# wq's guest rows in four loads of 9, 3, 7 and 5 rows from two queues, instead of eight loads of three rows from one

## The chip, the cores and the metric

The kernel runs on one core of a Trainium2 chip. The core has five engines that work side by side and meet at semaphores: TensorE (PE in the profile), VectorE (DVE), ScalarE (ACT), GpSimd (POOL) and SyncE (SP). Sixteen DMA engines bring data from HBM, the chip's main memory, into SBUF, the core's memory of 128 partitions. SP, ScalarE and GpSimd can each put loads into a queue of their own, and the same 16 DMA engines serve all queues. The metric is device time in microseconds (us), lower is better.

## The reference

One decode step of a transformer block for 4 sequences, all in float32: a layer norm whose scale and shift come from a condition c, attention over the last 2048 positions of a key and value cache, and a gated feed-forward part.

```python
mod = (_silu(c) @ w_mod).reshape(c.shape[0], 6, 1, -1)
sa, ca, ga, sb, cb, gb = (mod[:, n] for n in range(6))
h = _layernorm(x) * (1 + ca) + sa
# attention: 32 query heads, 8 key/value heads, window W = 2048, Dh = 128
q = (h @ wq) ...
o = softmax(q k^T * Dh ** -0.5) v
x = x + ga * (o @ wo)
h = _layernorm(x) * (1 + cb) + sb
x = x + gb * ((_silu(h @ w1) * (h @ w3)) @ w2)
```

With only 4 tokens there is little arithmetic for each weight and each cache entry: keys and values are 67 MB, the weights some 34 MB, and each of these bytes is used once.

## The kernel before, in words

**Memory.** `ring` is one SBUF tensor of three slots; a slot holds 128 partitions of 16384 floats, 8.39 MB. Every large load goes to a slot or a part of one, one row to each partition: w_mod_a (the part of w_mod that the first norm needs, with x and c), wq, seven loads kv_in (keys and values of one key/value head for all four sequences), wo_mod, the last head's keys with a quarter of wo (last_k_wo), its values (last_v), another quarter of wo, w1, w3, and w2 in four pieces of falling size.

**The order of the loads.** `load` (L174) issues a DMA on SP's queue unless told otherwise. SP issues w_mod_a, then the guest loads (below), then kv_in 0 to 6 and the rest in the order above. ScalarE issues one load, wq (L188), at the start. A load into a slot in use waits until the engines have read what lies there; `Program` (L44) finds such waits from the partitions and columns that each instruction touches, and gives every DMA a semaphore of its own.

**Guests.** wq as laid out on the host has 128 rows of 16384 floats. The last 240 columns (`GUESTS`) of every row are cut off, so that the load of wq has 128 rows of 16144 floats. The pieces that were cut off travel as an input of their own, `guests`: 24 rows of 6 x 240 = 1440 floats, in which a piece of six different partitions stands in one row. They are loaded into partitions 0 to 11 and 32 to 43 of the tile p_sb, which the softmax uses later; GpSimd clears those partitions first (L200). The eight loads before are written

```python
for m in range(2):
    for c in range(4):
        do("sync", "dma_start", guest[32 * m + c : 32 * m + 12 : 4], guests[12 * m + c : 12 * m + 12 : 4])
```

so each has the three partitions 32m + c, 32m + c + 4 and 32m + c + 8. In the matmuls with hT and wq (L306 to L315) the last 240 columns are taken from there: six matmuls with a matching slice `hg` of the transposed activations add the guests' share (twelve records in the trace, since a float32 matmul runs in two passes).

**Compute.** The first norm and its modulation wait for w_mod_a. Then come q (wq), and for each key/value head: scores on TensorE into s_ps, a maximum on VectorE (nm), the exponential on ScalarE (p_sb), transposes (bank), and the product with the values (o_ps). `project_out` multiplies by wo. At the end the feed-forward part runs twice through `ffn_in`, for w1 and for w3, and then through w2, whose last pieces are consumed as they land. The program's marked line splits it into two parts for its semaphores; the change lies in the first.

**Engines beside the stream.** On GpSimd there are five clearing instructions for tiles around the guest loads (p_sb, sc, hidT, qT, xs), and later one copy of x into xs, which waits for w_mod_a.

Of the kernel before, what the change touches and what calls it, by code (L numbers as in the profile page):

```python
# [147 lines left out]
def block_kernel(nc, w_mod_a, wq, guests, kv_in, wo_mod, last_k_wo, last_v, wo, w1, w3, w2, out):  # L148
# [5 lines left out]
    do = Program(nc)  # L154
# [19 lines left out]
    def load(dst, src, cuts=(0, 1), queue="sync"):  # L174
        step = src.shape[1] // cuts[-1]
        for lo, hi in zip(cuts[:-1], cuts[1:]):
            do(queue, "dma_start", dst[:, lo * step : hi * step], src[:, lo * step : hi * step])
        return dst[:, : src.shape[1]]
# [20 lines left out]
    p_all = sb("p_sb", NT * 512)  # L199
    do("gpsimd", "memset", p_all[:44], 0.0)  # L200
    guest = p_all[:44, : 6 * GUESTS]
    for m in range(2):
        for c in range(4):
            do("sync", "dma_start", guest[32 * m + c : 32 * m + 12 : 4], guests[12 * m + c : 12 * m + 12 : 4])
    kv[0] = load(slots[2], kv_in[0])
    sc = sb("sc", 4, 32)
    do("gpsimd", "memset", sc, 0.0)
# [98 lines left out]
    for half in range(2):  # L306
        qp = s_ps[half]
        for k in range(4):
            for i in range(4):
                at = ((half * 4 + i) * 4 + k) * 512  # L310
# [228 lines left out]
```

## Time and profile before

| | |
|---|---|
| time, median of 3 runs | 242.16 us (242.08 to 242.38) |
| span of the profiled execution, first to last instruction | 240.8 us |
| PE busy | 148.7 us (62%) |
| DVE busy | 56.3 us (23%) |
| ACT busy | 24.1 us (10%) |
| POOL busy | 4.5 us (2%) |
| mean granted TensorE clock | 0.865 |
| HBM read | 101.22 MB |

The page gives no time of its own for the profiled execution beside its span; the runs' median is 1.36 us above that span. The profile's lines name an instruction's source line, engine and operation, then the tile written and the tiles read. Nearly all compute has the line L59, that of the helper that records every operation, so groups are told apart by their tiles. A row of the timeline begins with its start and its length in us; what stands in square brackets is how long the engine was idle before it and what ended that. In the windows every engine has its busy time and, in brackets, its instructions; then come the granted clock, the mean busy share of the 16 DMA engines, and GB/s. A packet belongs to the window in which it starts, so a share over a short window can be a little off, and even above 1.

### The profile page before, as it was taken

The page shows a single profiled execution, that of the slowest core. Times are in us where ns is not written, and L with a number is a line of the kernel's source. Part 1 is how long each engine was busy: PE and PEld are TensorE (multiplying, and loading weights), DVE is VectorE, ACT ScalarE, POOL GpSimd, SP SyncE. Part 2 cuts the span into 40 slices and gives each one's busy share as a digit, 9 for nine tenths or more (in the row PEclk, how much of TensorE's full clock was granted, in tenths as well). Part 3 has the DMA queues.
Part 4 walks back from the last instruction along what each step waited for, and adds up shares of the span by engine and source line. Part 5 has one row for each costly group of instructions (what it writes and reads, how often), then busy time and mean ns, then how long its engine had stood idle before and what let it go on. Part 6 is the DMA issues. An engine that isn't in the chain of part 4 may idle for free.

```text
span 240.8 us, 2502 instructions
## 1 busy us (share of the span) xinstructions
PE 148.7 (62%) x1113; PEld 54.2 (22%) x1113; DVE 56.3 (23%) x141; ACT 24.1 (10%) x36; POOL 4.5 (2%) x12
## 2 busy tenths in 40 slices
PE   0000169982984962944867576667399719965876
PEld 0000133322322212201312222221042202422333
DVE  5000231034152024123132133130313104113210
ACT  2000000003003003001100300300200001320100
POOL 7000000000000000000000000000000000000000
PEclk9999997997696798879797799795759968995899
DMA  8999999999999999999999999999999999999994
GB/s 305 434 444 455 424 425 446 416 446 414 457 395 468 403 459 414 449 425 446 425 446 427 435 435 435 435 427 446 425 446 425 411 419 430 386 444 443 401 413 162
DMA packets 2937, 101.39 MB, mean 421 GB/s; under 512 B 472, under 2 KB 472, under 8 KB 880
## 3 DMA queue, kind: packets, MB, share of 16 engines
q1 hardware_dynamic: 2784, 92.99, 89.8%
q10 hardware_dynamic: 144, 8.27, 8.0%
q8 instruction: 8, 0.13, 0.2%
q14 instruction: 1, 0.01, 0.0%
HBM read 101.22 MB, written 0.03 MB: 420 GB/s over the span
## 4 chain that ended last, share of the span: by engine, by line
DMA 60%; PE 31%; DVE 5%; ACT 3%; issue 1%; ACTq 0%
DMA ring<-kv_in 33%; DMA ring<-w 16%; PE s_ps L59 14%; DMA ring<-w_mod_a 11%; PE bank L59 9%; PE o_ps L59 6%; DVE nm L59 3%; ACT p_sb L59 3%; PE a_ps L59 1%; DVE mod_a L59 0%; ACT work L59 0%; DVE p_sb L59 0%; DVE e L59 0%; DVE h L59 0%; DVE sq L59 0%
## 5 line engine op out<-in xcount | busy, mean ns | idle before, releaser
L59 PE MATMUL s_ps<-ring,qT 128*32 128x512 f32 x256 | 36.5, 722 | 20.3 <-DMA ring<-kv_in 13.3
L59 PE MATMUL bank<-ident,p_sb 128*128 128x128 f32 (+1 forms) x136 | 27.7, 353 | 30.8 <-ACT p_sb L59 30.7
L59 PE MATMUL o_ps<-ring,pT 128*16 128x512 f32 x256 | 38.4, 707 | 0.1
L59 PEld LDWEIGHTS bank<-ident,p_sb 128*128 128x128 f32 (+1 forms) x136 | 19.8, 178 | 52.5 <-ACT p_sb L59 31.7
L59 ACT ACTIVATE p_sb<-s_ps,nm 128x2048 f32<-128x2048 f32 (+1 forms) x11 | 16.5, 1501 | 139.7 <-DVE oT L59 104.1
L59 DVE TENSOR_REDUCE nm<-s_ps 128x1 f32<-128x2048 f32 x7 | 16.0, 2292 | 32.5 <-PE s_ps L59 32.5
L59 DVE COPY pT<-bank 128x64 f32<-128x64 f32 x32 | 7.2, 225 | 57.0 <-PE bank L59 57.0
L59 PEld LDWEIGHTS s_ps<-ring,qT 128*32 128x32 f32 x256 | 8.7, 129 | 46.9 <-issue 20.1
L59 PE MATMUL bank<-ident,xs 128*128 128x128 f32 x1 | 0.5, 476 | 27.8 <-POOL xs L59 27.8
L59 PE MATMUL s_ps<-ring,h2T 128*32 128x512 f32 (+1 forms) x64 | 9.0, 657 | 2.3 <-DMA ring<-w 2.3
L59 PE MATMUL s_ps<-ring,hT 128*32 128x512 f32 (+1 forms) x64 | 9.4, 705 | 0.0
L59 PEld LDWEIGHTS o_ps<-ring,pT 128*16 128x16 f32 x256 | 5.4, 99 | 11.9 <-issue 9.0
L59 DVE SCALAR_TENSOR_TENSOR o_own<-o_ps,rl,own 128x512 f32<-128x512 f32 x7 | 5.3, 751 | 11.1 <-PE o_ps L59 11.1
L59 PE MATMUL a_ps<-ring,oT 128*4 128x512 f32 x64 | 7.4, 592 | 0.0
L59 DVE TENSOR_REDUCE o_sum<-o_own 128x128 f32<-128x512 f32 x7 | 7.2, 1034 | 0.2
L59 PE MATMUL bank<-ring,sc 128*32 128x256 f32 (+1 forms) x64 | 6.9, 587 | 0.0
L59 PEld LDWEIGHTS bank<-ident,xs 128*128 128x128 f32 x1 | 0.2, 183 | 27.8 <-POOL xs L59 27.8
L59 DVE TENSOR_SCALAR e<-e 128x16 f32<-128x16 f32 x1 | 0.2, 175 | 23.3 <-ACT e L59 23.3
L59 DVE COPY qT<-bank 128x64 f32<-128x64 f32 x8 | 2.2, 280 | 12.4 <-PE bank L59 12.0
L59 DVE TENSOR_REDUCE mx<-s_ps 128x1 f32<-128x512 f32 x4 | 2.8, 692 | 9.0 <-PE s_ps L59 9.0
L59 PEld LDWEIGHTS s_ps<-ring,h2T 128*32 128x32 f32 x64 | 2.6, 130 | 7.3 <-issue 4.4
L59 PE MATMUL s_ps<-ring,hidT 128*32 128x64 f32 (+1 forms) x112 | 3.6, 274 | 0.3 <-DVE hidT L59 0.3
(97 smaller groups left out, 63.7 us busy)
## 6 DMA issues: line engine op xcount, KB each, us to landing
ring<-wq ACTq DMA_DIRECT2D x1, 8072.0 KB, 26.9
ring<-w SPq DMA_DIRECT2D x2, 3584.0 KB, 37.9
ring<-last_k_wo SPq DMA_DIRECT2D x1, 6144.0 KB, 30.1
ring<-last_v SPq DMA_DIRECT2D x1, 4096.0 KB, 39.5
ring<-w_mod_a SPq DMA_DIRECT2D x1, 2064.0 KB, 26.7
ring<-wo SPq DMA_DIRECT2D x1, 2048.0 KB, 41.8
ring<-w SPq DMA_DIRECT2D x1, 2048.0 KB, 43.1
ring<-w SPq DMA_DIRECT2D x1, 768.0 KB, 44.5
```

The costliest lines, as they stand in the source:

```text
L59: op = Op(engine, lambda: getattr(getattr(self.nc, engine), method)(*args, **kw), [])
```

## The change

The same 24 rows go from the same input to the same 24 partitions, in four loads: rows 0 to 8 and 9 to 11 (partitions 0 to 8 and 9 to 11) by SP, rows 12 to 18 and 19 to 23 (partitions 32 to 38 and 39 to 43) by GpSimd.

```diff
     guest = p_all[:44, : 6 * GUESTS]
-    for m in range(2):
-        for c in range(4):
-            do("sync", "dma_start", guest[32 * m + c : 32 * m + 12 : 4], guests[12 * m + c : 12 * m + 12 : 4])
+    for queue, at, lo, hi in (("sync", 0, 0, 9), ("sync", 0, 9, 12), ("gpsimd", 20, 12, 19), ("gpsimd", 20, 19, 24)):
+        do(queue, "dma_start", guest[at + lo : at + hi], guests[lo:hi])
     kv[0] = load(slots[2], kv_in[0])
```

On SP this is the start of the program; a row has the line, the tile written and the tensor read, and partitions x floats:

```order
 L59 DMA ring<-w_mod_a 128x4128
-L59 DMA p_sb<-guests 3x1440 x8
+L59 DMA p_sb<-guests 9x1440
+L59 DMA p_sb<-guests 3x1440
 L59 DMA ring<-kv_in 128x16384 x7
```

Six of SP's issues between w_mod_a and the first kv_in are gone, and the two that stay carry twelve of the rows, nine of them in one load.

On GpSimd the place is the clearing of tiles at the start:

```order
 L59 MEMSET ident 128x132
 L59 ISA
 L59 AFFINE_SELECT ident<-ident 128x128
 L59 MEMSET p_sb 44x2048
+L59 DMA p_sb<-guests 7x1440
+L59 DMA p_sb<-guests 5x1440
 L59 MEMSET sc 128x128
 L59 MEMSET hidT 128x504
```

Two loads stand behind the clearing of p_sb, for which they wait, and ahead of the other clearing instructions; GpSimd issued no load before. TensorE, VectorE and ScalarE have the same instructions as before in the same order; the matmul that reads the guests first now waits for four loads and not for eight.

## The prediction

> **What bounds the kernel now.** I read the page's transfer slices and queues first, because a kernel that reads 101 MB for four tokens is probably a stream:
>
> ```profile
> span 240.8 us, 2502 instructions
> DMA  8999999999999999999999999999999999999994
> GB/s 305 434 444 455 424 425 446 416 446 414 457 395 468 403 459 414 449 425 446 425 446 427 435 435 435 435 427 446 425 446 425 411 419 430 386 444 443 401 413 162
> DMA packets 2937, 101.39 MB, mean 421 GB/s; under 512 B 472, under 2 KB 472, under 8 KB 880
> q1 hardware_dynamic: 2784, 92.99, 89.8%
> q10 hardware_dynamic: 144, 8.27, 8.0%
> q8 instruction: 8, 0.13, 0.2%
> q14 instruction: 1, 0.01, 0.0%
> ```
>
> The 16 engines are busy from the first slice to the last but one. q1 is SP's queue, q10 is ScalarE's (wq alone), and nine packets carry instructions. So the time is that of one long stream, plus what follows it. The chain of waits, in order of time, shows the hand-overs:
>
> ```profile
> 65.50 1.89 PE o_ps L59 x16
> 67.41 38.51 DMA ring<-kv_in
> ...
> 190.94 38.54 DMA ring<-w
> 229.48 0.04 issue
> 229.52 3.71 PE s_ps L59 x20
> ...
> 237.49 1.31 PE s_ps L59 x64
> 238.80 0.03 issue
> 238.83 0.23 DVE p_sb L59
> ```
>
> A kv_in load takes 38.51 us from its issue to its landing, yet it carries 128x16384 floats, 8.39 MB, which is 19.3 us at the 435 GB/s of the slices. The other 19 us it stands in the queue behind the load before it. Compute may therefore be some 19 us late in the middle without leaving the engines idle. At the end it may not: w3 lands at 229.48 and TensorE starts on it at 229.52, and the last pieces of w2 are used just before 238.80. A later end of the stream is a later end of the kernel, one for one.
>
> Next: do all 16 engines end together? The windows over the end of the stream (columns as in the page; the last two are the busy share of the 16 engines and GB/s):
>
> ```profile
> 235.00:236.00 1.00, 1.00 (x12) 0.28 (x12) 0.00 (x0) 0.00 (x0) 0.00 (x0) 1.00 1.06 412
> 236.00:236.50 0.50, 0.50 (x8) 0.12 (x4) 0.00 (x0) 0.00 (x0) 0.00 (x0) 1.00 0.82 328
> 236.50:237.00 0.50, 0.50 (x33) 0.39 (x29) 0.00 (x0) 0.14 (x1) 0.00 (x0) 1.00 0.67 266
> 237.00:237.50 0.50, 0.47 (x35) 0.30 (x25) 0.00 (x0) 0.44 (x1) 0.00 (x0) 1.00 0.68 262
> 237.50:238.20 0.70, 0.70 (x50) 0.70 (x52) 0.00 (x0) 0.00 (x0) 0.00 (x0) 1.00 0.06 21
> ```
>
> They don't. From 236.5 to 237.5 the share is 0.67 to 0.68, and 11/16 is 0.69: five engines are done a microsecond early, and eleven run to the end. Every wide load gives each engine the same bytes, so what differs is the guest rows and the instruction packets. The count of small packets says how the guest rows lie. Of the 472 packets under 512 B, 128 are the rows of the 256 B output. The other 344 are 20 loads of 128 rows times 16, plus 8 guest loads times 3: one closing packet for each engine that a load uses. A load of three rows thus uses **three engines, one row each**. If the eight loads use the same three, these carry eight rows each. The other eight of the eleven fit the nine instruction packets (q8's eight take 0.2% of 16 x 240.8 us, about 0.96 us each), if each fell on another engine and one on an engine already late or already done. So I read: three engines late by guests, eight by instructions, five early.
>
> **The price of a row.** q1 took 89.8% of 16 x 240.8 us, 3460 us of engine time, for 92.99 MB: 26.9 kB per us and engine. A guest row is 1440 floats, 5760 B: **0.21 us**. Eight of them are 1.71 us.
>
> **The change, part by part.**
>
> ```profile
> 0.73 0.38 SPq L59 DMA_DIRECT2D ring<-w_mod_a  x1
> 3.23 5.67 SPq L59 DMA_DIRECT2D p_sb<-guests  x8
> 8.95 114.56 SPq L59 DMA_DIRECT2D ring<-kv_in  x7
> ...
> 1.41 1.80 POOL L59 MEMSET p_sb<- 44x2048 f32 x1
> ...
> 4.83 0.20 POOL L59 MEMSET xs<- 128x128 f32 x1
> 27.55 0.21 POOL L59 COPY xs<-ring 128x16 f32<-128x16 f32 x1 [22.52 <-DMA ring<-w_mod_a]
> ...
> 45.48 2.61 PE L59 MATMUL s_ps<-p_sb 44*32 44x240 f32 x12
> ```
>
> *SP issues.* Eight issues take 5.67 us, 0.71 each; six go, so the first kv_in is issued about 4.3 us sooner. Worth nothing: it queues behind w_mod_a, which lands at about 27 us (ScalarE and GpSimd wait for it until then).
>
> *GpSimd issues.* The trace has no load issued by GpSimd. From below they cost nothing, and I take twice SP's 0.71, 1.4 us. Behind them stand four memsets that end at 5.03, and then the copy of x, which waits 22.52 us for w_mod_a: only two issues of over 20 us together would be felt. The wait that GpSimd adds is for its own memset of p_sb, which SP waited for as well. TensorE reads the guests at 45.48; now it waits for four loads in place of eight, which stand in the queues where the eight stood, right behind w_mod_a or beside it. Nothing here is on the path.
>
> *w_mod_a.* GpSimd's rows now run beside w_mod_a and wq, so w_mod_a can land later by one row's time, 0.2 to 0.9 us. The 19 us of queueing cover that; without them it would count in full.
>
> *Which engine carries what.* This is the term that counts. The number of rows was the number of engines for 3 and for 128 (8 rows each on 16); I take 9, 3, 7 and 5 rows as one row on each of 9, 3, 7 and 5 engines. The three guest engines then carry about three rows for eight, 1.07 us less; they aren't alone at the end, so the kernel gains nothing by it. The rows land elsewhere. At most three guest engines and five early ones can take rows without harm, so of the nine-row load at least one row falls on one of the eight that are late by instructions, and an engine of these can get two, one from SP and one from GpSimd. Without any other effect the end moves by **+0.21 to +0.43**.
>
> The Trainium skill ("DMA: Bandwidth & Descriptors", "Why a DMA increments its semaphore by 16 and not by 1") has it that such a load takes the largest count up to 16 that divides its rows, on the lowest-numbered engines when SP issues it, and on consecutive ones from a moving cursor when GpSimd does. The 472 above agrees for 3 and 128; the GpSimd part no run here shows. With the cursor at 0, engines 3 to 8 would get two rows each, +0.43.
>
> *Where a row is written.* The old loads put rows c, c+4 and c+8 on the three engines; the new ones put neighbouring partitions 0, 1, 2, 3 on four engines at one moment, since the SP rows stand behind w_mod_a on all of them. In a wide load an engine fills eight partitions, always its own, and the engine shares of 0.9 and more say that the way into them is taken all the time. A foreign row has to go in beside the owner's stream. No row of the trace shows such a crossing, so I bound it: below, the partition side has room and the price stays 0.21 a row; above, four rows go abreast for each of two rows, 4 x 0.21 x 2 = 1.71. The least crossing has two parties, the guest and the owner: two rows at 0.43 are +0.86. With four abreast on one row and the other undisturbed it is 0.86 + 0.21 = 1.07. The total of the slices stays flat near 435 whatever load runs, so a limit exists, but not on which side; I choose the partition side and **+0.95**, between the last two.
>
> The Trainium skill ("SBUF — State Buffer", "Door 1: The DMA port swizzle") speaks against this change: four neighbouring partitions, with those 32 above, share one port of about 27 GB/s, and it gives 27.6 GB/s for a load into partitions 0 to 3 alone. By it the sum is the crossing's, by a port with room it is +0.43. No run shown so far tests it.
>
> **Sum.** Against the profiled span: 240.8 + 0.95 = 241.75. The median of the runs, 242.16, lies 1.36 above that span, which I take to be what surrounds it: **243.1 us**.
>
> **Rivals.**
>
> *No crossing.* The engine itself is the limit, and a row costs 0.21 us wherever it goes: 242.16 + 0.21 to 0.43, 242.4 to 242.6, say 242.5. For it: every row seen so far runs at the engine's rate. Against it: no row seen so far was written outside its engine's partitions as far as the trace tells.
>
> *Faster: the other eight weren't held by instructions.* If the eight small loads in q1 were what held them (their issues take SP until 8.9 us, and 24 rows with 24 closing packets stand ahead of kv_in), the end comes down to where the five early engines stop, about 236.5 instead of 237.6: -1.1 us, 241.1. It decides if the share of the engines falls from full to nothing at one time afterwards. Against it: nothing in q1 puts guest packets on more than three engines, and 3 + 8 counts out.
>
> *GpSimd's load isn't spread.* If its rows go to one engine, seven rows are 1.5 us on it, and should it be a late one with an SP row as well, +1.7: 243.9. It also covers the case that the change doesn't spread rows as it says. For it: no load of GpSimd is in the trace. Against it: every load there is was spread as far as its rows go.
>
> **How the numbers follow.** About 0.2% of this kernel, 0.48 us, is what a measurement can tell from no change. Crossing: 0.60, of which 0.04 stays under 0.48 us. No crossing: 0.28, within 0.2%. Faster: 0.05. Not spread: 0.07. That makes slower 0.56 + 0.07 = 0.63, the same 0.28 + 0.04 = 0.32, faster 0.05. The range reaches from the lower end of no crossing, 242.16 + 0.21, rounded down to 242.3, up to four abreast twice, 242.16 + 1.71, 243.9.
>
> **What would show it.** Right: w3 lands about 0.95 us after 229.48 and the tail behind it is unchanged; the share at the end of the stream still steps down; a new queue holds 12 rows; SP's issues end near 4.6 us. A shift of 0.2 to 0.4 is the engine's limit alone. No shift means that the rows found the early engines. The prediction is wrong altogether if the kernel ends early with all engines stopping together, or if the time outside the span changes from 1.36 us because a queue of GpSimd's comes with a cost of its own.

## The result, and the profile after

The changed kernel takes **243.59 us** (median of 5 runs, 243.5 to 243.75) against 242.16 us before: +1.43 us, ratio 1.0059 with a 95% interval of 1.0047 to 1.007. It is slower, clear of the 0.2% that can be told from no change, and inside the range of 242.3 to 243.9, about half as far again from the start as the 0.95 forecast. The profiled run took 243.54 us with a span of 242.2, so 1.3 us lie around the span as before.

The page of the changed kernel, slices and queues:

```profile
span 242.2 us, 2496 instructions
...
DMA  8999999999999999999999999999999999999993
GB/s 316 379 425 442 434 433 455 414 444 422 444 422 436 433 434 422 436 433 433 433 433 436 433 433 433 433 425 444 422 444 417 417 414 433 419 440 417 426 407 131
DMA packets 2977, 101.39 MB, mean 419 GB/s; under 512 B 512, under 2 KB 512, under 8 KB 920
...
q0 software_dynamic: 64, 0.07, 0.1%
```

The bytes are the same 101.39 MB, and the engines are as busy as before; they move 419 GB/s instead of 421. GpSimd's queue is q0 (twelve of its 64 packets are guest rows, the others have 4 B). The first difference by time is in the second and third slice, 6 to 18 us: 379 and 425 where 434 and 444 stood. The engines were busy there and moved less.

GpSimd's timeline shows its two loads (columns: start, length, what; in brackets the idle time before):

```profile
3.51 1.16 POOL L59 DMA_DIRECT2D p_sb<-guests  x2 [0.30 <-POOL p_sb L59]
4.67 0.23 POOL L59 MEMSET sc<- 128x128 f32 x1
...
28.95 0.21 POOL L59 COPY xs<-ring 128x16 f32<-128x16 f32 x1 [22.56 <-DMA ring<-w_mod_a]
```

Two issues took 1.16 us and held up nothing. The copy of x starts 1.40 us later than before (28.95 against 27.55), because w_mod_a lands later. The chain at the end, in order of time:

```profile
194.15 36.88 DMA ring<-w
231.03 0.04 issue
231.07 3.71 PE s_ps L59 x20
...
239.04 1.16 PE s_ps L59 x64
240.20 0.02 issue
240.22 0.24 DVE p_sb L59
```

w3 lands at 231.03 instead of 229.48, 1.55 us later; the work behind it is the same to within 0.2 us. So the change cost time in the stream alone. The windows over the end of the stream (the last two columns are the busy share of the 16 engines and GB/s):

```profile
237.00:237.50 0.50, 0.50 (x12) 0.13 (x4) 0.00 (x0) 0.00 (x0) 0.00 (x0) 1.00 1.07 401
237.50:238.00 0.50, 0.50 (x8) 0.12 (x4) 0.00 (x0) 0.00 (x0) 0.00 (x0) 1.00 0.71 275
238.00:238.50 0.50, 0.50 (x30) 0.35 (x26) 0.00 (x0) 0.10 (x1) 0.00 (x0) 1.00 0.40 152
238.50:239.00 0.50, 0.50 (x37) 0.34 (x26) 0.00 (x0) 0.49 (x1) 0.00 (x0) 1.00 0.08 29
```

The eleven that ended together are gone. The share falls in steps, and after 238.5 it is 0.08, about one engine of sixteen (0.06).

### The profile page after: what moved, and what is told of

Same layout as the page of the kernel before. It is cut to its first block, busy times and chain, and to the rows that moved or that the text cites. A ratio compares the mean times of both kernels' runs of the same rounds, so it can differ in the third digit from the quotient of the medians.

```text
span 242.2 us, 2496 instructions
## 1 busy us (share of the span) xinstructions
PE 149.5 (62%) x1113; PEld 54.7 (23%) x1113; DVE 55.7 (23%) x141; ACT 24.1 (10%) x36; POOL 5.5 (2%) x14
## 2 busy tenths in 40 slices
DMA packets 2977, 101.39 MB, mean 419 GB/s; under 512 B 512, under 2 KB 512, under 8 KB 920
## 4 chain that ended last, share of the span: by engine, by line
DMA 60%; PE 31%; DVE 5%; ACT 3%; issue 1%; ACTq 0%
DMA ring<-kv_in 17%; DMA ring<-wo_mod 16%; DMA ring<-w 15%; PE s_ps L59 13%; DMA ring<-w_mod_a 12%; PE bank L59 9%; PE o_ps L59 6%; DVE nm L59 3%; ACT p_sb L59 3%; PE a_ps L59 2%; DVE mod_a L59 0%; ACT work L59 0%; DVE p_sb L59 0%; DVE e L59 0%; DVE h L59 0%
## 5 line engine op out<-in xcount | busy, mean ns | idle before, releaser
L59 PE MATMUL s_ps<-ring,qT 128*32 128x512 f32 x256 | 35.1, 697 | 17.5 <-DMA ring<-kv_in 12.1
L59 PEld LDWEIGHTS bank<-ident,p_sb 128*128 128x128 f32 (+1 forms) x136 | 20.3, 182 | 52.6 <-ACT p_sb L59 31.7
L59 PE MATMUL a_ps<-ring,oT 128*4 128x512 f32 x64 | 9.1, 709 | 2.1 <-DMA ring<-wo_mod 2.1
L59 DVE COPY oT<-bank 128x16 f32<-128x16 f32 x8 | 1.3, 167 | 10.8 <-PE bank L59 10.8
```

The source lines that it names most:

```text
L59: op = Op(engine, lambda: getattr(getattr(self.nc, engine), method)(*args, **kw), [])
```

## The experiments

Each was timed against the kernel before on the same chip, whose median there was 242.23 to 242.29 us. The diffs stand against the changed kernel, long lines cut with `...`; where one shows only added lines, they stand in place of the change's two. In them `guest` is the tile of 44 partitions.

### Are three engines held by guests and eight by something else?

The four guest loads are taken out and nothing is put in their place:

```diff
-    for queue, at, lo, hi in (("sync", 0, 0, 9), ...
-        do(queue, "dma_start", guest[at + lo : at + hi], guests[lo:hi])
```

> The guest loads are left out, so the last 240 columns of q are computed from zeros. If eight engines are late by instruction packets alone, the end hardly moves (0 to -0.1 us, 242.0 to 242.2 us), though 0.14 MB less is loaded, and the share of the 16 engines over the last microsecond of the stream falls from 11/16 to 8/16. If the guest rows held all eleven, the end comes down by about 1.1 us, 241.0.

242.1 us, ratio 0.9997 (0.9988 to 1.0005): no change. The windows of this kernel:

```profile
236.00:236.50 0.50, 0.50 (x8) 0.13 (x4) 0.00 (x0) 0.00 (x0) 0.00 (x0) 1.00 0.73 270
236.50:237.00 0.50, 0.50 (x34) 0.40 (x30) 0.00 (x0) 0.15 (x1) 0.00 (x0) 1.00 0.50 197
237.00:237.50 0.50, 0.46 (x35) 0.30 (x25) 0.00 (x0) 0.43 (x1) 0.00 (x0) 1.00 0.38 148
```

The 0.67 of before has become 0.50, eight of sixteen, and then 0.38, at the same end time. The times at which w3 landed on each engine are clearer than the shares: here eight engines end between 228.95 and 229.47 and the other eight by 228.25; in the kernel before eleven end between 229.15 and 229.48 and five by 228.34. The reading holds: three engines were late by guests and eight without any. The records of single packets in the trace show what holds these: an instruction packet of 16 KB takes its engine about 1.0 us, and the stream's packet right behind it is about 0.5 us longer than its fellows. Seven of these packets and the one of 8 KB run before w3 lands, which makes the eight; the last one of 16 KB runs at 236.

### SP's part and GpSimd's part alone

In the first the rows 12 to 23 go back to four loads of three rows from SP, in the second the rows 0 to 11 do:

```diff
-... ("gpsimd", 20, 12, 19), ("gpsimd", 20, 19, 24)
+    for c in range(4):
+        do("sync", "dma_start", guest[32 + c : 44 : 4], guests[12 + c : 24 : 4])
```

```diff
-... ("sync", 0, 0, 9), ("sync", 0, 9, 12)
+    for c in range(4):
+        do("sync", "dma_start", guest[c : 12 : 4], guests[c : 12 : 4])
```

> Rows 0 to 11 in SP's two loads of 9 and 3; rows 12 to 23 in four loads of three rows as before, from SP. Theory 'a row costs its time wherever it is written': the engines of the 9-row load get one row of 0.21 us each, the end moves by +0.2, 242.4 us, and the engine records of the first kv_in rows stay at their usual length. Theory 'crossing': the twelve rows of SP cost more than their bytes (in the changed kernel the first kv_in rows were some 0.4 us longer on engines that carry no guest row), the end moves by +0.4 to +0.7, 242.6 to 242.9. Theory 'GpSimd's queue is the cost': nearly nothing here, 242.2 to 242.4.

> Rows 12 to 23 in GpSimd's two loads of 7 and 5; rows 0 to 11 in four loads of three rows as before, from SP. Theory 'a row costs its time': +0.2, 242.4 us. Theory 'GpSimd's queue is the cost': the stream is slower between 8 and 18 us (slices 2 and 3 of the page near 379 and 425 GB/s, as in the changed kernel, against 434 and 444), the end moves by +0.4 to +1.0, 242.6 to 243.2. Theory 'crossing': GpSimd's rows cross as well, about half of the change's 1.43, 242.7 to 242.9.

SP's part: 242.58 us, +0.33 over the 242.25 of before beside it (ratio 1.0013, 1.0004 to 1.0022). GpSimd's part: 242.81 us, +0.56 (1.0027, 1.0017 to 1.0037). Both cost something. By time alone SP's +0.33 lies between the theories; the packet records further down decide it. GpSimd's part has the loss in the early slices, as the page of that kernel shows:

```profile
GB/s 288 399 426 429 503 390 477 393 466 401 466 404 456 412 457 412 456 415 445 423 445 426 434 434 434 434 426 445 423 445 415 418 418 428 406 426 441 416 411 140
```

399 and 426 against 434 and 444. That can be GpSimd's queue or where its rows go. The two parts add up to 0.89 of the 1.43.

### Is it GpSimd's queue?

All four loads of 9, 3, 7 and 5 rows from SP:

```diff
-(("sync", 0, 0, 9), ("sync", 0, 9, 12), ("gpsimd", 20, 12, 19), ("gpsimd", 20, 19, 24))
+(("sync", 0, 0, 9), ("sync", 0, 9, 12), ("sync", 20, 12, 19), ("sync", 20, 19, 24))
```

> The four loads of 9, 3, 7 and 5 rows to the same partitions, all issued by SP. Theory 'GpSimd's queue is the cost': most of the loss goes, 242.4 to 242.7 us. Theory 'crossing': the loss stays or grows, since all 24 rows are then written at one moment, 243.2 to 244.0. Theory 'a row costs its time': three rows on engines 0 to 4, at most two or three on an engine that is late anyway, +0.4 to +0.6, 242.6 to 242.8.

243.42 us, ratio 1.005 (1.0037 to 1.0064): +1.17, so without GpSimd most of the loss is there. The page of this kernel has it in the fifth slice, 24 to 30 us, where SP's guest rows run:

```profile
GB/s 287 439 442 449 346 465 411 446 422 443 433 435 422 433 434 422 435 422 454 411 454 414 443 411 465 422 446 422 443 422 422 433 403 433 413 433 435 403 416 149
```

346 where the kernel before has 424, and the slices of 6 to 18 us are whole again at 439 and 442. The loss doesn't need GpSimd's queue; it goes where the loads go.

### Is it the partitions?

This pair differs in nothing but the partitions. Three loads of eight rows by SP, the same source rows, the same number of rows for each load; in one, load c goes to every fourth partition from c, in the other to eight neighbours:

```diff
+    for c in range(3):
+        do("sync", "dma_start", guest[c : 32 : 4], guests[8 * c : 8 * c + 8])
```

```diff
+    for c in range(3):
+        do("sync", "dma_start", guest[8 * c : 8 * c + 8], guests[8 * c : 8 * c + 8])
```

> The 24 rows in three loads of eight, all by SP, load c to the partitions c, c+4, ..., c+28: eight engines with three rows each, and if an engine owns four neighbouring partitions, each row in its engine's own. The rows then stand in other partitions than the matmul takes them from, so the last 240 columns of q are other numbers. Theory 'crossing': no engine waits for another, the first kv_in rows keep their 2.42 us, and the end moves by three rows on the engines among these eight that are late by instructions, +0.5 to +0.65, 242.7 to 242.9 us (less if all late ones lie higher). Theory 'several engines at once are the cost, wherever they write': the first kv_in rows are longer by about 1 us as when SP issued all of 9, 3, 7 and 5, 243.2 to 243.6.

> As e5_eight_step4 with the same source rows, engines and number of rows, but load c goes to the partitions 8c to 8c+7 next to one another (here too the last 240 columns of q are other numbers). Only the partitions differ. Theory 'crossing': the first kv_in rows are longer by about 1 us on all engines, and the end lies 0.6 to 1.2 us above e5_eight_step4. Theory 'source rows or number of engines': both kernels take the same time within 0.2 us.

Every fourth partition: 242.49 us, ratio 1.0003 (0.9988 to 1.0017), not to be told from before. Eight neighbours: **243.46 us**, ratio 1.0048 (1.0035 to 1.0062). 0.97 us for another choice of partitions: that neighbouring partitions are the cost is shown. What makes them dear is not separated further. If a load's rows are dealt to the engines in turn, then in every dear form rows go outside the partitions that their engine fills in a wide load, and several of them go to neighbours at once; no kernel has one without the other, and "crossing" stands for both below. The first kernel came out cheaper than expected (242.7 to 242.9). In its trace w3 lands after 229.48 on only three engines, at 229.76 to 229.88, so probably more of the engines late by instructions are without guest rows than I allowed for. In the second kernel the kv_in rows grew by 0.54 us (the table below), not by the 1 us expected.

A third kernel issues the third load of the cheap form from GpSimd:

```diff
+    for queue, c in (("sync", 0), ("sync", 1), ("gpsimd", 2)):
+        do(queue, "dma_start", guest[c : 32 : 4], guests[8 * c : 8 * c + 8])
```

> As e5_eight_step4, but the third of the loads is issued by GpSimd (here too the last 240 columns of q are other numbers). If GpSimd's load takes the same eight engines, nothing crosses. Theory 'GpSimd's queue itself costs': the stream loses 0.2 to 0.4 us between 8 and 10 us (the second slice near 400 GB/s and not 435), and the end is 0.2 to 0.4 above e5_eight_step4. Theory 'only crossing costs': the second slice stays near 435 and the time is that of e5_eight_step4 within 0.15.

242.56 us, ratio 1.0011 (1.0002 to 1.002), 0.07 above its twin. The second slice came out between the two expectations, and the time on the side of "only crossing":

```profile
GB/s 280 414 430 444 524 348 521 350 511 359 511 361 500 369 490 380 481 391 478 391 478 394 467 402 467 402 459 413 456 402 435 435 405 435 412 419 442 419 405 130
```

Slices are short enough here to be moved by where packets start (524 and 348 stand side by side), so the packet records are the better witness.

### Twice the rows

The same pair, with its three loads issued a second time to the partitions 32 above:

```diff
+    for at in (0, 32):
+        for c in range(3):
+            do("sync", "dma_start", p_all[at + 8 * c : at + 8 * c + 8, : 6 * GUESTS], guests[8 * c : 8 * c + 8])
```

and with `p_all[at + c : at + 32 : 4, ...]` for the cheap form.

> e6_eight_in_a_row with its three loads issued a second time, to partitions 32 to 55: 48 rows, all next to one another (the last 240 columns of q are other numbers here too). Theory 'crossing': the price goes with the number of crossing rows, so the first kv_in rows of engines without guests are longer by about 1.1 us instead of 0.54, and the end lies 0.6 to 1.2 above e6_eight_in_a_row, 244.0 to 244.7 us. Theory 'a fixed cost of the first such load': the time stays within 0.7 (three rows of 0.22) of e6_eight_in_a_row only because of the bytes, and the first kv_in rows stay at +0.54.

> e5_eight_step4 with its three loads issued a second time, to the partitions 32 above: 48 rows, each in its engine's own partitions if the engine owns four neighbours and the four 32 above them (the last 240 columns of q are other numbers here too). Theory 'crossing': the first kv_in rows keep 2.42 us, and the end moves by what three more rows cost an engine of the lower eight that is late by instructions, +0.4 to +0.66 over e5_eight_step4, 242.9 to 243.2. Theory 'guest rows cost the same wherever they go': e9 and e10 take the same time.

Neighbours: 244.33 us, ratio 1.0087 (1.0074 to 1.0101). Every fourth partition: 243.32 us, ratio 1.0045 (1.0031 to 1.0059), 0.83 above its single form and so a little over the expected 0.66. Of the neighbours' 0.87 over their single form, then, the rows alone explain nearly all: the distance between the two forms stayed at 1.01 us, where it was 0.97 with half the rows. The first kv_in rows grew by 0.81 us, neither the 1.1 of one theory nor the 0.54 of the other. How the price of crossing grows with the number of rows stays open.

What each kernel's packet records say, in us. The first column is the median length of the first eight kv_in rows (64 KB) to start, which are mostly those of engines with few or no guest rows of SP; then come the mean lengths of a guest row of SP, and of a w_mod_a row that starts between 8.3 and 9.4 us, where GpSimd's first load runs:

```
kernel                            kv_in row   guest row (SP)   w_mod_a row
before                              2.42         0.220           0.615
the change                          2.86         0.311           0.698
SP's part alone                     2.70         0.275           0.625
GpSimd's part alone                 2.42         0.221           0.803
all by SP                           3.50         0.376           0.618
eight rows, every fourth            2.42         0.220           0.615
eight rows, neighbours              2.96         0.271           0.615
every fourth, one load by GpSimd    2.42         0.220           0.619
twice, neighbours                   3.23         0.303           0.615
twice, every fourth                 2.42         0.220           0.617
```

Read it by columns. Wherever every row goes to every fourth partition, the guest rows and the kv_in rows have their usual lengths of 0.220 and 2.42, and w_mod_a's rows theirs within 0.004, whoever issues the loads. Wherever SP writes neighbours, its guest rows grow in the mean (in the kernel with eight neighbours the first twelve keep 0.22 and the later ones take up to 0.44), and so do the rows of **other** engines that run beside them: 2.42 to 2.86 in the change, to 3.50 with all loads on SP. With SP's part alone, whose larger load uses nine engines, thirteen of the sixteen first kv_in rows took 2.57 to 2.72. GpSimd's rows do the same to w_mod_a's rows at 8 to 9 us, while they themselves hardly grow (0.223 in GpSimd's part alone, 0.227 in the change). Why engines that only run beside such a row slow down, no run here shows.

### The last 0.5 us

The two parts add up to 0.89 of 1.43. The landing times of w3 on each of the 16 engines, from the trace's completion records, show what is left:

```
before        227.76 227.80 227.92 228.29 228.34 229.15 229.20 229.21 229.29 229.30 229.36 229.42 229.44 229.44 229.47 229.48
the change    228.72 229.32 229.34 229.41 229.59 229.85 229.89 229.95 229.96 230.05 230.07 230.12 230.13 230.38 230.41 231.03
change again  229.06 229.09 229.37 229.45 229.79 230.02 230.33 230.41 230.47 230.48 230.52 230.62 230.65 230.68 230.72 231.13
SP's part     228.22 228.24 228.49 228.59 228.84 229.43 229.53 229.74 229.80 229.81 229.87 229.90 229.91 229.94 229.99 230.06
GpSimd's part 228.27 228.49 228.63 228.86 229.04 229.45 229.50 229.71 229.84 229.85 229.86 229.92 229.97 230.07 230.16 230.23
```

In the change one engine ends alone, 0.62 behind the next; in the two parts alone the last two are 0.07 apart. Followed back through the loads, this engine falls 0.97 us behind between the landings at 87 and at 107, when the instruction packet of 8 KB (q14) runs at 89.1: the packet takes 0.32 us, and the kv_in row behind it is 0.66 longer than its fellows. It was already among the late ones, 1.69 us behind the first engine. In the kernel before, the packet of that kind hit an engine that was 0.70 behind. Is that set by the program or by chance? The changed kernel was run once more:

> The changed kernel once more, as it is. In its first profile the instruction packet near 89 us seemed to fall on an engine that an instruction packet had delayed at 44 us, and this engine ended 0.6 us behind the next. If the engine of that packet is set by the program, the gap of about 0.6 us at the end comes back and the time is 243.5 to 243.7 again; if it is chance, the gap is mostly gone and some runs are near 243.0.

243.7 us, ratio 1.0057 (1.0044 to 1.0069), and 0.41 between the last two engines: the gap came back, a third smaller, and no run was below 243.49. That speaks for the program. In this second profile the other engines were late too (the next to last at 230.72, where the first profile has 230.41), so how the 0.5 divides isn't settled.

The other traces have the same step of 0.97 at that packet, and they suggest more. The engine that it meets stood 0.57 us behind the first one without guests, 1.20 with three rows on each of eight engines in the cheap form, and 1.85 with six; three rows are 0.66 and six 1.32. With SP's and GpSimd's part alone it stood at 0.75 and 1.06, in the change at 1.69 and 1.31. So it may be one and the same engine in all kernels, one of those that get guest rows in the new loads, and then the change makes it late by its rows and not by another choice of engine. That is an estimate from landing times; the trace doesn't name the engines, and no kernel was tried that moves the packet, so this part stays open.

## Why the prediction was right, and where it was off

*The bound and the tail*: right. The stream set the time, and its end moved the kernel's end nearly one for one (w3 +1.55, span +1.4).

*Eleven engines, three by guests and eight by instructions*: right: without guests eleven late engines become eight at the same end time. Of the nine instruction packets the one to spare is the last, which runs after w3 has landed.

*The price of a row*, 0.21: the records say 0.220, for every row of the loads to every fourth partition.

*SP's and GpSimd's issues are worth nothing*: as forecast, the work behind GpSimd's two issues had over 20 us to spare. Their lengths were taken too long, 0.33 each on SP and 0.58 on GpSimd where the prediction has 0.71 and 1.4; SP's ended at 3.89 and not at 4.6. A load to neighbours is issued faster: three loads of eight rows took SP 1.03 us, and 2.12 to every fourth partition. w_mod_a landed 1.40 us later and not 0.2 to 0.9; the kv_in loads queue behind it, and the engines stayed busy.

*Crossing*: the choice of the partition side over the engine's own limit was right, and the runs show it by the pair of eight rows. Its size and its form were off. The prediction let only the guest row and the owner of the partition pay. The runs show that rows of other engines grow as well, by 0.44 us on a 2.42 us row in the change. SP's and GpSimd's part cost 0.33 and 0.56, about 0.9 together; that the forecast 0.95 lies so near is luck in part, since it was chosen between two counts of parties that no run bears out. That the total fell inside the range owes much to the range's upper end, four rows abreast twice.

The Trainium skill ("SBUF — State Buffer", "Door 1: The DMA port swizzle") puts four neighbouring partitions and those 32 above on one port of about 27 GB/s. The pair agrees in direction: 0.220 us a row in the cheap form and 0.271 in the dear one. It doesn't agree in size: an estimate from that figure, four rows of 5760 B abreast on one port, is 0.85 us a row, and the longest row of the pair took 0.44. That engines on other ports are slowed too doesn't follow from the sharing of one port.

*The term that was missing*: about 0.5 us by which one engine ends alone. The sum took it that the instruction packets leave eight different engines equally late, as before; in the change the one of 8 KB met an engine that was late already.

*The rivals.* No crossing would have kept the kv_in rows at 2.42 us in the change; they were 2.86. Faster is out, since the eight were late without guests too. GpSimd's load not spread is out as well: the seven rows of its first load start between 8.20 and 9.00 us in the change and take 0.22 to 0.27 each, and one engine would have needed 1.5 us for them.

## What to carry to other kernels

In a kernel bound by its loads, the end is set by the DMA engines that are last, and a look at the busy share over the last microsecond tells how many they are: bytes taken from the others gain nothing (here all guest loads, 0.14 MB). A small load that runs beside a full stream should, as far as these runs go, be written to every fourth partition, one row to an engine; neighbouring partitions cost 0.97 us for 24 rows of 5760 B, more than four times what one of the rows takes.

## What was not expected of the hardware

A crossing write slows engines that take no part in it: with all 24 rows on SP in loads of 9, 3, 7 and 5, the first 64 KB rows, mostly of engines without guest rows, took 3.50 us instead of 2.42. And an instruction packet of 16 KB costs its engine about 1.5 us (1.0 for itself and 0.5 on the packet behind it), where 16 KB of the stream cost it 0.6; seven such packets and one of 8 KB (0.97) make the eight engines that are last without guests.
